# FNet and GeGLU layers on one core: the first row tiles' statistics and loads in another order, and the last rows' additions tied in turn

## The chip, the cores and the metric

One core of one Trainium2 chip. The metric is the device time of one execution in microseconds, the median of several runs. Profile times count from the first instruction of the profiled execution.

## The reference

Four layers over x (2048 rows of 512, fp32), each with a residual and a layer norm ahead of it: Fourier mixing, a GeGLU feed-forward layer, mixing again, feed-forward again.

```python
def _A_ref(x, dft_seq_re, dft_seq_im, dft_hid_re, dft_hid_im):
    a = jnp.einsum("bsd,ed->bse", x, dft_hid_re)
    b = jnp.einsum("bsd,ed->bse", x, dft_hid_im)
    return jnp.einsum("ts,bse->bte", dft_seq_re, a) - jnp.einsum("ts,bse->bte", dft_seq_im, b)
def _B_ref(x, w_gate, w_up, w_down):
    return (_gelu(x @ w_gate) * (x @ w_up)) @ w_down
x = A_x
x = x + _A_ref(_layernorm(x), ...)
x = x + _B_ref(_layernorm(x), ...)
x = x + _A_ref(_layernorm(x), ...)
x = x + _B_ref(_layernorm(x), ...)
```

The matrices are cosines and sines for the mixing (`ws` along the 2048 rows, `wh` along the 512 columns) and 512 x 1792 weights for the feed-forward layers.

## The kernel before

**Products.** Every fp32 operand is divided into a high part (rounded to fp32r by ScalarE, `split`, L126) and a low part (what is left, by VectorE, L128). A product is three matmuls (`mm3`, L166 to L168): high by high, high by low, low by high. Block products are saved in the manner of Strassen, which gives the many names (A11, S1, T2 and so on), and the additions for them run on VectorE (`minus` L154, `plus` L157) beside the matmuls.

**The opening.** In the first mixing layer the work goes over 16 half row tiles j and, in each, over 4 blocks b of output rows: `fore` calls `six` for each (j, b), and `six` takes the next divided 256 KB tile of `ws` (tile 4j + b), issues six matmuls of 512 columns with row tile j (24 a row tile), and then runs one entry of a work queue (`step`). Row tile j must by then be loaded (`x_load`, L194), normalised and divided. Normalising row tile i (`norm_terms`): VectorE's statistics (`bn_stats`, L531), mean and variance (L533), + EPS (L534), GpSimd's power -0.5 (L535), VectorE's shift (L536); then ScalarE writes the normalised row (`normed`, L572), and its halves are divided like the rest (`split_side`, which calls `split`). Row tiles 0 to 7 give the first eight j ("11"), and rows 8 to 15 are used for the other eight.

Row tile 0 has a function of its own, `first_tile` (statistics L1404, mean L1405, + EPS L1406, power L1407, subtraction L1408, high part L1411, low part L1412). It puts the division of ws tiles 0, 1 and 2 (`split_next`) around them. `first_made` and `issue_after` tie the divisions of tiles 1 and 2 behind row tile 0's own high and low part: `issue_after(ins)` keeps an instruction behind `ins` in the queue of the same engine.

Row tiles 1 to 7 come from the work queue: `opening(k)` asks for the load of row k + 1 and normalises row k, `first_parts(k)` divides it; after each pair stand as many pauses as `OPEN_GAPS` says, from the third pair on entries for rows 8 and up in their place. `opening(2)` (`SECOND_AT`) also asks for row 8. The statistics of a row are tied behind the + EPS step of the row before and the shift of the row before that (`terms_made`).

**Loads.** All loads of x and ws in the opening go through SyncE's queue (SP): x by L194, ws by `load_next`, L302. `split_next` keeps six ws tiles loaded ahead of the one that it divides (RAW), and `take`, which `six` calls, keeps seven divided ahead of the one used (AHEAD). An SP load uses one of eight semaphores in turn and waits until the load eight before it has landed.

**The order of the queues.** The code gives the dependences and an order of priority. The tile framework, with `schedule_with_timeline_sim`, plans each engine's queue at build on a timing model whose constants `machine_as_traced` sets; of what the model holds ready, it takes the earliest in the code. On the chip each queue runs as it was planned.

**The end.** In the last feed-forward layer `last_rows` computes the last product for four tiles of 128 rows: 21 matmuls of 256 columns for each (seven `mm3`), one addition to a tile `straight[n]` (loaded by L1292 from a scratch tensor, alternately on SP's and ScalarE's queue), and the store of the sum, 64 rows on SP's queue and 64 on ScalarE's (L1310).

Of the kernel before, what the change touches and what calls it, by code (L numbers as in the profile page):

```python
# [12 lines left out]
ALU = mybir.AluOpType  # L13

P = 128
S, D, F = 2048, 512, 1792
# [5 lines left out]
NT = TB // P  # L22
# [6 lines left out]
WARM = 11  # L29
OPEN_MORE = 0  # L30
SECOND_AT = 2
OPEN_GAPS = 1, 2, 1, 1, 1, 1, 1
NEAR = 2, 6
EARLY = 2
PACE = 9
# [26 lines left out]
def fnet_geglu(ctx: ExitStack, tc: tile.TileContext, x_in, ws, wh, whc, wgu, wdc, out):  # L62
    nc = tc.nc
# [57 lines left out]
    def f32(ap):  # L121
        return ap.bitcast(F32)

    def split(src, hi, lo):
        with behind(0):
            nc.scalar.activation(hi, src, AF.Copy)  # L126
        with behind(1):
            nc.vector.tensor_tensor(lo, src, f32(hi), op=ALU.subtract)  # L128

    first_made = []  # L130

    def behind(i):
        return tc.issue_after(first_made[i]) if first_made else nullcontext()
# [22 lines left out]
    def plus(out, a, b):  # L156
        nc.vector.tensor_tensor(out, a, b, op=ALU.add)  # L157
# [6 lines left out]
    def mm3(ps, a, b, start, stop):  # L164
        (ah, al), (bh, bl) = a, b
        nc.tensor.matmul(ps, ah, bh, start=start, stop=False, skip_group_check=True)  # L166
        nc.tensor.matmul(ps, ah, bl, start=False, stop=False, skip_group_check=True)  # L167
        nc.tensor.matmul(ps, al, bh, start=False, stop=stop, skip_group_check=True)  # L168
# [123 lines left out]
    def load_next():  # L292
        n = stream["loaded"]
        dtype, addresses, _, _ = items[n]
        raws[n] = []
        assert n not in needs or needs[n] in outside
        for a in addresses:
            t = sb.get(dtype)
            to = t if dtype == F32 else f32(t)
            if len(a.shape) == 3:  # L300
                to = to.rearrange("p (h c) -> p h c", h=2)
            stream["last"] = nc.sync.dma_start(to, a)  # L302
            raws[n].append(t)
        stream["loaded"] += 1

    def too_far(n):

        return items[n][2] is whole and n > stream["used"] + items[n][3]

    def split_next():  # L310
        n = stream["split"]
        while stream["loaded"] <= min(n + RAW, len(items) - 1) and not too_far(stream["loaded"]):
            load_next()
        parts[n] = items[n][2](*raws.pop(n))
        stream["split"] += 1

    def take():
        n = stream["used"]
        while stream["split"] < len(items):
            at = stream["split"]  # L320
            _, _, make, need = items[at]
            if too_far(at) or make is not whole and at > n + AHEAD + stream["more"]:
                break
            if make is not whole and need and need not in cs and at > n:
                break
            split_next()
        stream["used"] += 1
        return parts.pop(n)
# [183 lines left out]
    known, terms_made = {}, []  # L512

    def row_of(layer, i, mixed):
        x = fresh.pop(("mixed", i) if mixed else i, None)
        if x is None:
            x = (x_load_mixed if mixed else x_load)(layer, i)
        return x

    def norm_terms(layer, i, x, junk):  # L520

        pool = spool if layer == 0 else kpool
        rstd = pool.tile([P, 1], F32, name="rstd")
        shift = pool.tile([P, 1], F32, name="shift")
        if layer == 0:
            st = spool.tile([P, 6], F32, name="st")
            with ExitStack() as behind:
                for back, which in (1, 0), (2, 1):
                    if len(terms_made) >= back:
                        behind.enter_context(tc.issue_after(terms_made[-back][which]))  # L530
                nc.vector.bn_stats(st, x)  # L531
            mv = spool.tile([P, 2], F32, name="mv")
            nc.vector.bn_aggr(mv, st)  # L533
            added = nc.vector.tensor_scalar_add(rstd, mv[:, 1:2], EPS)  # L534
            nc.gpsimd.tensor_tensor(rstd, rstd, power, op=ALU.pow)  # L535
            made = nc.vector.scalar_tensor_tensor(shift, mv[:, 0:1], -1.0, rstd, op0=ALU.mult, op1=ALU.mult)  # L536
            terms_made.append((added.ins, made.ins))
        else:

            total = spool.tile([P, 1], F32, name="total")  # L540
            mean = spool.tile([P, 1], F32, name="mean")
            nc.scalar.activation(junk, x, AF.Copy, accum_out=total)  # L542
            nc.scalar.activation(mean, total, AF.Copy, scale=-1.0 / D)
            nc.scalar.activation(junk, x, AF.Square, bias=mean, accum_out=rstd)  # L544
            nc.gpsimd.tensor_scalar(rstd, rstd, 1.0 / D, EPS, op0=ALU.mult, op1=ALU.add)  # L545
            nc.gpsimd.tensor_tensor(rstd, rstd, power, op=ALU.pow)
            nc.scalar.activation(shift, mean, AF.Copy, scale=rstd)
        return rstd, shift
# [13 lines left out]
    def norm_begun(layer, i, mixed=False):  # L562

        x = row_of(layer, i, mixed)
        begun[layer, i] = x, known.pop((layer, i), None) or norm_terms(layer, i, x, junk)
# [516 lines left out]
    def geglu(w, layer):  # L1082
# [123 lines left out]
        def prepared(name, k):  # L1206

            if (name, k) in bs:
                return
            if name in ("S1", "S2") and len(h4[k]) == 4:  # L1210
                second_made(k)
            if name == "S2" and k >= MADE:
                fourth_made(k)
            t = h4[k][PLACE[name]]
            bs[name, k] = split_slot(t)
            sb.put(t)
# [60 lines left out]
        def halves(view, c):  # L1277
            return view[..., c * 64:(c + 1) * 64]
# [15 lines left out]
        def last_rows():  # L1294

            ks = range(NP)
            ts = [take()[0] for _ in ks]
            for k in ks:
                prepared("A22", k)
            to = xs[layer + 1, w * 2].rearrange("(n r) (p e) -> n r p e", r=P, e=P)  # L1300
            for n in range(NT):
                ps, v = ps8.get(), straight[n][:, :D // 2]
                for t, k in zip(ts, ks):
                    weights = (u[:, n * P:(n + 1) * P] for u in bs["A22", k])
                    mm3(ps[:, :D // 2], weights, (t[:, h] for h in half), k == 0, k == NP - 1)
                into = v.rearrange("r (p c e) -> r p c e", p=NT, e=32)
                plus(into, into, ps[:, :D // 2].rearrange("r (c p e) -> r p c e", p=NT, e=32))
                for i, engine in enumerate((nc.sync, nc.scalar)):
                    r = slice(i * 64, (i + 1) * 64)
                    engine.dma_start(halves(to[n, r], 1), v[r].rearrange("r (p e) -> r p e", e=64))  # L1310

        before_mix = w == 1 and layer < 3
# [41 lines left out]
        if last:  # L1354
            last_rows()
# [10 lines left out]
    ps = ps8.get()  # L1366
# [6 lines left out]
    def x_ahead(i):  # L1373
        if i < NS and i not in loaded:
            loaded.add(i)
            fresh[i] = x_load(0, i)
# [9 lines left out]
    def opening(k):  # L1386

        def run():
            x_ahead(k + 1)
            if k == SECOND_AT:  # L1390
                x_ahead(NK)
            first_norm(0, k)
        return run
# [7 lines left out]
    def first_tile():  # L1401

        x, st, mv, rstd = fresh.pop(0), *(spool.tile([P, n], F32, name=name) for name, n in (("st", 6), ("mv", 2), ("rstd", 1)))
        nc.vector.bn_stats(st, x)  # L1404
        nc.vector.bn_aggr(mv, st)  # L1405
        nc.vector.tensor_scalar_add(rstd, mv[:, 1:2], EPS)  # L1406
        nc.gpsimd.tensor_tensor(rstd, rstd, power, op=ALU.pow)  # L1407
        nc.vector.tensor_scalar(x, x, mv[:, 0:1], None, op0=ALU.subtract)  # L1408
        split_next()
        p = zparts["11", 0] = sb.get(F32R)  # L1410
        high = nc.scalar.activation(p[:, half[0]], x[:, half[0]], AF.Copy, scale=rstd)  # L1411
        made = nc.vector.scalar_tensor_tensor(p[:, half[1]], x[:, half[0]], rstd, f32(p[:, half[0]]), op0=ALU.mult, op1=ALU.subtract)  # L1412
        terms_made.append((made.ins, made.ins))
        first_made.extend((high.ins, made.ins))
        split_next()
        split_next()
        first_made.clear()

        def whole_row():
            z = za[0] = sb.get()  # L1420
            nc.scalar.activation(z, x, AF.Copy, scale=rstd)
            sb.put(x)
        return whole_row
# [6 lines left out]
    for n in range(NK - 1):  # L1430
        queue += [firsts.pop(0), firsts.pop(0)]
        queue += [seconds.pop(0) if n >= SECOND_AT else None for _ in range(OPEN_GAPS[n])]
    queue += seconds
# [77 lines left out]
```

## Time and profile before

| | before |
|---|---|
| time, median of 3 runs | 1589.22 us (1588.48 to 1590.95) |
| profiled execution, device time | 1589.32 us |
| profiled execution, span | 1587.3 us |
| VectorE busy, share of the span | 79% |
| ScalarE busy | 55% |
| GpSimd busy | 16% |
| DMA, mean over the span | 269 GB/s |
| granted TensorE clock | 0.999 |

The span runs from the first to the last instruction; the device time has 2.0 us more around it. A matmul's recorded duration overlaps with the next one's, so the distance from start to start is what counts. A row of the timeline may merge several instructions of a kind (x2, x9); its duration then runs from the start of the first to the end of the last. The bracket behind a row gives the idle time of the engine before it and what ended it. A DMA's row is its issue; landings are listed apart.

### The profile page before, as it was taken

Reading aid. Unit: us, or ns where it says so; the run is one execution under the profiler, and the core shown is the slowest. Engines: PE = TensorE matmul, PEld = TensorE weight load, DVE = VectorE, ACT = ScalarE, POOL = GpSimd, SP = SyncE. Lnnn points to the kernel's source line nnn. Section 1 sums busy time; section 2 is a strip of 40 time slices with the busy share of each in tenths; the row PEclk is TensorE's granted clock in tenths of the full one; section 3 lists DMA queues with packets and bytes.
Section 4 is the critical chain, followed back from the end, with each engine's and each line's share of the span. In section 5 each row is a group of like instructions: output and inputs, shape, how many; then the busy total and the mean of one; then the engine's idle time right before and its main releaser. Section 6 shows DMA issues by size and latency. Waiting matters only on the chain.

```text
span 1587.3 us, 23208 instructions
## 1 busy us (share of the span) xinstructions
PE 1579.0 (99%) x7000; PEld 1307.6 (82%) x7000; DVE 1250.1 (79%) x2174; ACT 875.4 (55%) x1714; POOL 253.6 (16%) x445
## 2 busy tenths in 40 slices
PE   9999999999999999999999999999999999999998
PEld 7888888888888888888888888888888888888887
DVE  8999999889699795566969997869985458754475
ACT  7864574645676652746768444566546435433361
POOL 2200324311465201230031000021002000000001
PEclk9999999999999999999999999999999999999999
DMA  9946989987999999996976785789998967896463
GB/s 360 332 150 232 361 270 362 335 286 259 328 344 345 297 329 301 288 331 221 310 238 217 270 229 172 233 283 309 279 327 239 297 198 238 293 289 197 135 197 81
DMA packets 257660, 427.04 MB, mean 269 GB/s; under 512 B 33344, under 2 KB 89408, under 8 KB 256512
## 3 DMA queue, kind: packets, MB, share of 16 engines
q1 hardware_dynamic: 228560, 333.28, 66.2%
q0 software_dynamic: 26544, 91.51, 15.7%
q8 instruction: 55, 0.90, 0.2%
q10 hardware_dynamic: 2432, 0.79, 0.2%
q14 instruction: 69, 0.57, 0.1%
HBM read 335.02 MB, written 90.44 MB: 268 GB/s over the span
## 4 chain that ended last, share of the span: by engine, by line
PE 96%; DVE 2%; DMA 2%; issue 0%; ACT 0%; SPq 0%; DVEq 0%; ACTq 0%
PE p L166 32%; PE p L167 32%; PE p L168 32%; DMA s<-ws 1%; DVE s L128 1%; DVE s L154 0%; DMA s<-x 0%; DVE s L157 0%; DVE xwide L154 0%; ACT s L126 0%; DVE wide L154 0%; SPq L302 0%; SPq L194 0%; ACT s L572 0%; DVE wide L157 0%
## 5 line engine op out<-in xcount | busy, mean ns | idle before, releaser
L167 PE MATMUL p<-s,s 128*128 128x512 f32 x2326 | 899.8, 388 | 0.0
L168 PE MATMUL p<-s,s 128*128 128x512 f32 x2326 | 887.6, 388 | 0.0
L166 PE MATMUL p<-s,s 128*128 128x512 f32 x2326 | 872.5, 388 | 2.0 <-ACT s L126 1.5
L126 ACT ACTIVATE s<-s 128x512 fp32r<-128x512 f32 (+1 forms) x868 | 487.4, 608 | 319.8 <-DVE s L154 108.7
L128 DVE TENSOR_TENSOR s<-s,s 128x512 fp32r<-128x512 f32 (+1 forms) x868 | 546.0, 669 | 58.2 <-ACT s L126 54.0
L166 PEld LDWEIGHTS p<-s,s 128*128 128x128 f32 x2326 | 436.7, 188 | 94.2 <-ACT s L126 3.4
L167 PEld LDWEIGHTS p<-s,s 128*128 128x128 f32 x2326 | 436.8, 188 | 89.7 <-DVE s L128 0.5
L168 PEld LDWEIGHTS p<-s,s 128*128 128x128 f32 x2326 | 436.6, 188 | 89.4
L157 DVE TENSOR_TENSOR s<-s,p 128x512 f32<-128x512 f32 (+1 forms) x293 | 196.2, 682 | 189.6 <-PE p L168 109.5
L154 DVE TENSOR_TENSOR s<-s,s 128x512 f32<-128x512 f32 (+1 forms) x414 | 249.8, 623 | 2.8 <-DMA s<-ws 0.9
L161 ACT ACTIVATE s<-p 128x512 f32<-128x512 f32 x252 | 146.9, 592 | 147.0 <-PE p L168 142.0
L1079 ACT ACTIVATE s<-s 128x512 f32<-128x512 f32 x112 | 70.3, 629 | 121.5 <-DVE s L157 121.0
L247 POOL DMA_DIRECT2D x<-wide x16 | 10.4, 660 | 374.7 <-DVE wide L157 374.7
L285 POOL DMA_DIRECT2D wb<-s x84 | 45.9, 548 | 100.2 <-ACT s L126 73.3
L1093 DVE TENSOR_TENSOR s<-s,s 128x512 f32<-128x512 f32 x84 | 57.9, 689 | 1.9
L126 ACT ACTIVATE s<-xwide 128x512 fp32r<-128x512 f32 (+1 forms) x52 | 31.0, 613 | 27.5 <-DVE xwide L157 10.0
L572 ACT ACTIVATE s<-s,shift,rstd 128x512 f32<-128x512 f32 x55 | 44.0, 807 | 3.9 <-DVE shift L536 3.2
L157 DVE TENSOR_TENSOR s<-s,s 128x512 f32<-128x512 f32 (+1 forms) x68 | 40.1, 591 | 5.0 <-DMA s<-wgu 3.3
L545 POOL TENSOR_SCALAR rstd<-rstd 128x1 f32<-128x1 f32 x48 | 14.2, 296 | 179.9 <-ACT junk L544 179.1
L285 POOL DMA_DIRECT2D wc<-s x42 | 30.1, 718 | 74.8 <-ACT s L126 53.2
L128 DVE TENSOR_TENSOR s<-xwide,s 128x512 fp32r<-128x512 f32 (+1 forms) x52 | 35.0, 682 | 7.1 <-ACT s L126 7.0
L542 ACT ACTIVATE junk<-s 128x512 f32<-128x512 f32 x45 | 28.1, 623 | 18.7 <-DMA s<-x 18.4
(105 smaller groups left out, 526.8 us busy)
## 6 DMA issues: line engine op xcount, KB each, us to landing
s<-ws SPq DMA_DIRECT2D x348, 256.0 KB, 5.1
s<-wb SPq DMA_DIRECT2D x294, 256.0 KB, 5.4
s<-wc SPq DMA_DIRECT2D x196, 256.0 KB, 4.5
wb<-s POOLq DMA_DIRECT2D x98, 256.0 KB, 5.6
s<-wp SPq DMA_DIRECT2D x56, 256.0 KB, 4.0
wc<-s POOLq DMA_DIRECT2D x49, 256.0 KB, 5.7
s<-x SPq DMA_DIRECT2D x45, 256.0 KB, 5.3
xwide<-x SPq DMA_DIRECT2D x43, 256.0 KB, 8.0
```

The source lines that it names most:

```text
L126: nc.scalar.activation(hi, src, AF.Copy)
L128: nc.vector.tensor_tensor(lo, src, f32(hi), op=ALU.subtract)
L154: nc.vector.tensor_tensor(out, a, b, op=ALU.subtract)
L157: nc.vector.tensor_tensor(out, a, b, op=ALU.add)
L161: nc.scalar.activation(v, src, AF.Copy)
L166: nc.tensor.matmul(ps, ah, bh, start=start, stop=False, skip_group_check=True)
L167: nc.tensor.matmul(ps, ah, bl, start=False, stop=False, skip_group_check=True)
L168: nc.tensor.matmul(ps, al, bh, start=False, stop=stop, skip_group_check=True)
L285: nc.gpsimd.dma_start(to, t)
L572: nc.scalar.activation(z, x, AF.Identity, bias=shift, scale=rstd)
L1079: nc.scalar.activation(t, g, AF.Gelu_apprx_tanh)
L1093: nc.vector.tensor_tensor(t, t, v, op=ALU.mult)
```

## The change

In the opening:

- `x_ahead` in `opening(k)` asks for row k + 2 (`X_AHEAD`) where it asked for row k + 1.
- The pauses after the first two pairs are 2 and 1 where they were 1 and 2.
- In `first_tile`, ws tile 1 is divided ahead of row tile 1's statistics, + EPS and shift (`norm_begun(0, 1)`, which were the first part of `opening(1)`); the statistics are tied behind tile 1's low part (`last_low`), and the low parts of the next two ws tiles, 2 and 3, behind row tile 1's + EPS step. `first_tile` now divides four ws tiles (0 to 3) and not three; `opening(1)` finds the terms begun and only writes the normalised row.

At the end:

- Each addition of `last_rows` is tied behind the one before it on VectorE.
- The rows of the first three tiles are stored whole by one DMA (ScalarE's, SP's and again ScalarE's queue), the last tile's as before in two halves.

```diff
-OPEN_GAPS = 1, 2, 1, 1, 1, 1, 1
+X_AHEAD = 2
+OPEN_GAPS = 2, 1, 1, 1, 1, 1, 1
...
         with behind(1):
-            nc.vector.tensor_tensor(lo, src, f32(hi), op=ALU.subtract)
-
-    first_made = []
+            last_low[0] = nc.vector.tensor_tensor(lo, src, f32(hi), op=ALU.subtract).ins
+
+    first_made, last_low = [], [None]
...
-                plus(into, into, ps[:, :D // 2].rearrange("r (c p e) -> r p c e", p=NT, e=32))
-                for i, engine in enumerate((nc.sync, nc.scalar)):
-                    r = slice(i * 64, (i + 1) * 64)
+                with tc.issue_after(made.ins) if n else nullcontext():
+                    made = nc.vector.tensor_tensor(into, into, ps[:, :D // 2].rearrange("r (c p e) -> r p c e", p=NT, e=32), op=ALU.add)
+                engines = (nc.sync, nc.scalar) if n == NT - 1 else ((nc.scalar, nc.sync)[n % 2],)
+                for i, engine in enumerate(engines):
+                    r = slice(i * P // len(engines), (i + 1) * P // len(engines))
                     engine.dma_start(halves(to[n, r], 1), v[r].rearrange("r (p e) -> r p e", e=64))
...
         def run():
-            x_ahead(k + 1)
+            x_ahead(k + X_AHEAD)
             if k == SECOND_AT:
                 x_ahead(NK)
             first_norm(0, k)
...
         made = nc.vector.scalar_tensor_tensor(p[:, half[1]], x[:, half[0]], rstd, f32(p[:, half[0]]), op0=ALU.mult, op1=ALU.subtract)
-        terms_made.append((made.ins, made.ins))
         first_made.extend((high.ins, made.ins))
+        split_next()
+        terms_made.append((last_low[0], last_low[0]))
+        norm_begun(0, 1)
+        first_made[1] = terms_made[-1][0]
         split_next()
         split_next()
         first_made.clear()
```

## The prediction

> **What bounds the kernel now.** I read first the busy times of the page, then TensorE's waits, then the timeline of the opening and of the end.
>
> ```profile
> span 1587.3 us, 23208 instructions
> ...
> PE 1579.0 (99%) x7000; PEld 1307.6 (82%) x7000; DVE 1250.1 (79%) x2174; ACT 875.4 (55%) x1714; POOL 253.6 (16%) x445
> ```
>
> TensorE's waits (total us, times, longest):
>
> ```profile
> PE p L166 <- ACT s L126: 1.5, 3, 0.8
> ```
>
> TensorE is the bound: idle 8.3 us of 1587.3, and the three waits of its matmuls for a high part (L126) sum to 1.5. So what the change can win lies in a few places: stalls in the opening, one later, and the stretch after the last matmul. The opening's timeline (start, duration, engine, line; the bracket is idle time before it):
>
> ```profile
> 7.52 0.62 PE L168 MATMUL p<-s,s 128*128 128x512 f32 x2
> ...
> 8.02 0.73 PE L166 MATMUL p<-s,s 128*128 128x512 f32 x2
> ...
> 9.97 0.40 PE L167 MATMUL p<-s,s 128*128 128x512 f32 x1
> ...
> 11.57 0.39 PE L168 MATMUL p<-s,s 128*128 128x512 f32 x1
> ...
> 12.71 0.50 PE L166 MATMUL p<-s,s 128*128 128x512 f32 x1 [0.75 <-ACT s L126]
> ...
> 23.54 0.39 PE L168 MATMUL p<-s,s 128*128 128x512 f32 x1
> ...
> 24.30 0.50 PE L166 MATMUL p<-s,s 128*128 128x512 f32 x1 [0.37 <-ACT s L126]
> ...
> 29.20 0.84 PE L168 MATMUL p<-s,s 128*128 128x512 f32 x3
> 29.99 0.50 PE L166 MATMUL p<-s,s 128*128 128x512 f32 x1
> 30.32 0.40 PE L167 MATMUL p<-s,s 128*128 128x512 f32 x1
> ```
>
> Durations overlap, so I count from start to start. Two matmuls take 0.62 where one takes 0.39: starts lie 0.23 apart. 11.57 to 12.71 is 1.14, so 0.91 is lost; the first gap after a stall is longer (29.99 to 30.32 is 0.33 to 0.34), 0.11 more. 23.54 to 24.30 loses 0.53, and 0.11 again. Before 29.99 it is 0.11 (the third of x3 starts at 29.20 + 0.45 = 29.65, the next was due at 29.88), then 0.11. At 8.02, due at 7.97, it is 0.05 and 0.11 (0.73 for two). **The opening can give 0.16 + 1.02 + 0.64 + 0.22 = 2.04 us, no more.** The stalls at 12.71, 24.30 and 29.99 stand before the first matmuls of row tiles 1, 3 and 4 (24 matmuls, 5.45 us, a row tile).
>
> **Row tile 1's statistics.** What made row tile 1 late:
>
> ```profile
> 5.88 0.62 ACT L126 ACTIVATE s<-s 128x512 fp32r<-128x512 f32 x1
> 6.00 0.48 DVE L1412 SCALAR_TENSOR_TENSOR s<-s,rstd,s 128x256 fp32r<-128x256 f32 x1 [0.40 <-ACT s L1411]
> ...
> 6.55 0.70 DVE L531 BATCH_NORM_STATS2 st<-s 128x6 f32<-128x512 f32 x1
> ...
> 7.16 0.67 DVE L128 TENSOR_TENSOR s<-s,s 128x512 fp32r<-128x512 f32 x1
> ...
> 7.75 0.17 DVE L533 BATCH_NORM_AGGREGATE mv<-st 128x2 f32<-128x6 f32 x1
> 8.00 0.69 DVE L128 TENSOR_TENSOR s<-s,s 128x512 fp32r<-128x512 f32 x1
> ...
> 8.61 0.15 DVE L534 TENSOR_SCALAR rstd<-mv 128x1 f32<-128x1 f32 x1
> ...
> 8.84 0.93 POOL L535 TENSOR_TENSOR rstd<-rstd,power 128x1 f32<-128x1 f32 x1 [3.41 <-DVE rstd L534]
> ...
> 10.49 0.63 ACT L126 ACTIVATE s<-s 128x512 fp32r<-128x512 f32 x1 [1.21 <-DMA s<-ws]
> 10.52 0.14 DVE L536 SCALAR_TENSOR_TENSOR shift<-mv,rstd 128x1 f32<-128x1 f32 x1
> ...
> 11.03 0.80 ACT L572 ACTIVATE s<-s,shift,rstd 128x512 f32<-128x512 f32 x1
> ```
>
> The chain is statistics, mean and variance, + EPS, the power on POOL, the shift, the normalised row on ScalarE (L572), its high half (L126), TensorE. Low parts (L128) stand between its short DVE steps. The change adds no instruction here. The low part of ws tile 1 goes first: its high part ends at 6.50, DVE is free at 6.48, so it starts at about 6.55 and the next 0.61 later (6.55 to 7.16 now). Then nothing stands between: statistics 7.16, mean about 7.87, + EPS 8.07. Behind that step, which was at 8.61, the low parts of tiles 2 and 3 now queue: about 8.15, where tile 2's was at 8.00, and 0.6 later. Tile 2's ends at 8.85, and its matmuls begin at 9.97 (the fifth L167), so this is hidden by 1.1 us, and a loss is excluded. POOL's power runs 8.3 to 9.2, and the shift comes behind tile 3's low part at about 9.4, 1.1 earlier than 10.52. ScalarE is idle from 9.28 (10.49 - 1.21) to 10.49, so L572 runs 9.6 to 10.4; its high half (0.40) follows at once, or behind tile 5's high part at 11.1 to 11.5. TensorE wants it at 11.80, or 11.64 without the 8.02 stall. **The first stall goes, 1.0 to 1.2 us**; tile 1's low part, 0.6 earlier, fills 8.02. What hides the moved work is that idle 1.21 of ScalarE. Were the row to stand behind the high parts of tiles 5 and 6, it would cost two of 0.62 again and the stall would stay.
>
> The Trainium skill ("TensorE: Matmul & The Clock Gate", Part 1: The HAM clock gate) says that ScalarE and VectorE take their queues strictly in order. By that rule L572 cannot pass a high part that waits for its load (10.49), and everything hangs on the planned order, as in rival A. This trace shows the wait of 1.21 us, but no ready instruction held behind it.
>
> **x rows two ahead.** What is late next is row tile 3:
>
> ```profile
> 13.17 0.33 SPq L194 DMA_DIRECT2D s<-x  x1
> ...
> 13.86 0.33 SPq L302 DMA_DIRECT2D s<-ws  x1
> ...
> 14.31 4.57 ACT L126 ACTIVATE s<-s 128x512 fp32r<-128x512 f32 x9
> ...
> 14.96 5.25 DVE L128 TENSOR_TENSOR s<-s,s 128x512 fp32r<-128x512 f32 x9 [0.28 <-ACT s L126]
> ...
> 20.11 0.69 DVE L531 BATCH_NORM_STATS2 st<-s 128x6 f32<-128x512 f32 x1
> ...
> 23.85 0.40 ACT L126 ACTIVATE s<-s 128x256 fp32r<-128x256 f32 x1
> ```
>
> The loads there (KB each, median us to landing):
>
> ```profile
> s<-x SPq DMA_DIRECT2D x15, 256.0 KB, 5.4
> ```
>
> SP issues one 256 KB load each 0.68 us (13.17, 13.86), and they land 5.4 later; row 3 landed at about 18.6. In the code its load stands behind ws tile 16 (asked for in row 2's opening); now, asked for in row 1's, behind tile 13. Three places of SP's queue are 2.0 us, and tiles 14 to 16 land 0.68 later each. That is hidden: ScalarE's nine high parts end at 18.88 with tile 16, which row tile 4 wants at 29.99. Rows 4 and 8, now asked for together behind tile 17, move 2.7 ahead and 0.7 back. The statistics of row 3 waited for nine operations of L128 (5.25, 0.58 each); two of these, the low parts of tiles 15 and 16, come behind it in code order, so with the row there it can start 1.15 earlier. Bounds: 0 (the same place in DVE's queue) and 2.0 (the whole lead); I take 1.15, from those rows. Its high half then ends at 24.25 - 1.15 = 23.1, where a TensorE without stalls wants it at 24.30 - (0.05 + 0.11 + 0.91 + 0.11 + 0.53) = 22.59. A stall of 0.5 is left, TensorE stands 1.15 earlier than now, and row tile 4 must come 1.15 earlier too, which its lead of 2.7 allows. With 0.1 to 0.2 of the 0.22 at 29.99 **the opening gives 1.3 us, bounds 0 and 2.04**. The gap of two, moved ahead, only shifts row 2's step by one group of six matmuls; row 2's tile is not late now: nothing.
>
> **The last rows.** The end:
>
> ```profile
> 1582.40 0.75 DVE L157 TENSOR_TENSOR s<-s,p 128x256 f32<-128x256 f32 x2 [3.80 <-PE p L168]
> ...
> 1582.86 1.47 ACTq L1310 DMA_DIRECT2D out<-s  x2
> ...
> 1583.53 0.80 ACTq L1310 DMA_DIRECT2D out<-s  x1
> ```
>
> The landing of these two issues of ACT's queue (last column, us), in their order:
>
> ```profile
> out<-s ACTq DMA_DIRECT2D x1, 64.0 KB, 2.9
> ...
> out<-s ACTq DMA_DIRECT2D x1, 64.0 KB, 2.7
> ```
>
> Stretches of the end (the last columns are TensorE's clock, the DMA engines' share, GB/s):
>
> ```profile
> 1581.50:1583.00 1.50, 0.87 (x8) 0.66 (x6) 0.59 (x2) 0.00 (x0) 0.00 (x0) 1.00 1.02 225
> 1583.00:1584.50 1.50, 0.00 (x0) 0.00 (x0) 0.16 (x1) 0.00 (x0) 0.00 (x0) 1.00 0.84 183
> ```
>
> DVE waits 3.80 us and then does two additions: row 2's had been ready for some 2.3 us (84 narrow matmuls, 0.12 each, 21 a row), but stood behind row 3's. Tied in turn, it runs at about 1580.1 and its one 128 KB store is issued then; row 3's runs at 1582.40 as now, and its halves, the last ones, issue at 1582.86 and not 1583.53. By the issue the last landing moves from 1583.53 + 2.7 to 1582.86 + 2.9, 0.47 earlier. But the DMA engines are at a share of 1.02 where row 2's bytes are pulled ahead to, and 0.84 just after; the same bytes drain, and only the unused 0.16 x 1.5 = 0.24 is surely to be had. Below: 0, if row 2's whole store holds up row 3's half on ACT's queue. I take **0.3**, nearer to 0.24.
>
> The Trainium skill ("DMA: Bandwidth & Descriptors", Queues, rings and completion order) says that the engines serve their queues in turn and each ring in order. By it the drain decides, and the end gains 0.24, not 0.47; the share of 1.02 agrees.
>
> **The sum.** 1589.32 (the profiled execution: its span of 1587.3 and 2.0 around it) - 1.3 - 0.3 = 1587.7. The median of the runs shown, 1589.22, is 0.1 lower, less than their spread. 0.2% is 3.2 us, about what a measurement of this kernel can tell from no change.
>
> **Rivals.** A, *the rows stay late* (0.24): the order of each queue is planned at build on a model of the chip, not taken from the code. If row 1's L572 is still planned behind tiles 5 and 6, or row 3's statistics behind the same low parts, the stall at 24.30 takes back what 12.71 gave. For it: row 3's statistics started 1.5 us after landing. Against: the code now puts both ahead. Opening 0.2, end 0.3: 1588.8. That the end keeps its order as well, so that the change does nothing: 1589.3 (0.06).
>
> B, *slower, by a new plan where VectorE has no reserve* (0.10):
>
> ```profile
> 880.00:922.00 42.00, 41.65 (x184) 34.22 (x183) 42.00 (x71) 21.73 (x37) 2.16 (x4) 1.00 0.73 236
> ```
>
> ```profile
> 920.34 0.47 PE L166 MATMUL p<-s,s 128*128 128x512 f32 x1 [0.35 <-ACT s L126]
> ```
>
> In the third layer DVE is busy 42.00 of 42.00 us, and TensorE stalls once (0.35 by its bracket; by starts about 0.5, as 0.37 was 0.53 at 24.30). 42.00 / 71 is 0.6 an operation. If the changed opening makes the planner put other DVE work ahead of what TensorE wants, each such operation costs 0.6. Three undo the gain; eight cost 4.8 and give 1587.7 + 4.8 = 1592.5, over 0.2% slower. For it: no reserve. Against: the code there is unchanged, and the stretch moves as a whole with TensorE.
>
> C, *all of it goes* (0.10): 2.04 in the opening, 0.47 at the end, the 0.5 at 920.34: 1589.32 - 3.0 = 1586.3. Even that is 0.18%.
>
> **How the numbers follow.** Forecast 0.50, A 0.24, nothing 0.06, B 0.10, C 0.10. Predicted 1587.7. Range 1586.3 to 1590.2: from C to the unchanged time and about 1 us, for the runs' spread and the first of B's operations; the rest of B and the lowest of C are left out. Faster by over 0.2% means under 1586.0, below what all stalls hold: 0.06, for the spread around C. Slower means over 1592.4, B alone: 0.10. Within: 0.84.
>
> **What would show it.** Right: the gap before 12.71 is gone and row tile 3 starts at about 23.1; statistics of row 3 at about 19.0; row 2's last addition alone near 1580.1 on the old scale, the last issue 0.46 us after the last addition's start, a span near 1585.7. Wrong: row 1's L572 still at 11.0; matmuls late at each row tile; new waits of TensorE between 880 and 922 us; a last landing as late after the last matmul as now, which would mean that the drain alone sets the end.

## The result, and the profile after

The changed kernel takes 1594.62 us (median of 18 runs, 1590.62 to 1596.88) against 1590.25 (18 runs, 1588.25 to 1594.34): ratio 1.0023, interval 1.0016 to 1.0029. The forecast was 1587.7, up to 1590.2. The profiled execution took 1595.86 us with a span of 1593.7, 1.2 above its median; that of before was 0.9 below its own, so the two profiles differ by 6.4 where the medians differ by 4.4.

The page of after: span and busy times.

```profile
span 1593.7 us, 23203 instructions
...
PE 1582.0 (99%) x7000; PEld 1308.6 (82%) x7000; DVE 1249.9 (78%) x2174; ACT 874.2 (55%) x1714; POOL 260.7 (16%) x445
```

Where the time went is read from the start of the same matmul in both traces:

| matmul (of 7000) | before, us | after, us | after is late by |
|---|---|---|---|
| 118, near row tile 4 | 29.99 | 28.38 | -1.61 |
| 770 | 177.93 | 176.30 | -1.63 |
| 900 | 207.60 | 210.24 | 2.64 |
| 2500 | 570.32 | 574.88 | 4.56 |
| 4000 | 910.32 | 915.72 | 5.40 |
| 5500 | 1251.02 | 1256.97 | 5.95 |
| 6999 | 1582.09 | 1587.97 | 5.88 |
| last landing | 1586.18 | 1592.42 | 6.24 |

The opening gained 1.6 us and TensorE kept it for 150 us. Then 4.3 us went between 176 and 210, 1.9 by 575, 1.4 by 1257, and 0.3 at the end. Of the 1.4, two gaps that before doesn't have, of 0.55 ending at 852.9 and of 0.43 ending at 1127.7, make 1.0.

A single profile of each kernel is a small sample. Four profiled kernels have the opening of before (before, e1, e9, e14 below): their matmul 118 starts at 29.45 to 30.59, mean 30.07. In the six with the changed opening (after, e2, e7, e11, e13, e17) it starts at 28.27 to 29.27, mean 28.64. By these the opening gained 1.4 us.

**The opening**, after: the timeline of TensorE, then of VectorE and ScalarE (start, duration).

```profile
11.33 0.39 PE L169 MATMUL p<-s,s 128*128 128x512 f32 x1
11.56 0.39 PE L167 MATMUL p<-s,s 128*128 128x512 f32 x1
...
22.44 0.40 PE L167 MATMUL p<-s,s 128*128 128x512 f32 x1
...
27.66 0.39 PE L169 MATMUL p<-s,s 128*128 128x512 f32 x1
28.38 0.50 PE L167 MATMUL p<-s,s 128*128 128x512 f32 x1 [0.33 <-ACT s L127]
```

```profile
7.10 0.69 DVE L532 BATCH_NORM_STATS2 st<-s 128x6 f32<-128x512 f32 x1
...
9.52 0.82 ACT L573 ACTIVATE s<-s,shift,rstd 128x512 f32<-128x512 f32 x1 [0.21 <-DVE shift L537]
...
17.34 0.69 DVE L532 BATCH_NORM_STATS2 st<-s 128x6 f32<-128x512 f32 x1
```

Row tile 1 starts at 11.56 without a gap (before 12.71 behind one of 0.91), row 3's statistics at 17.34 (20.11), row tile 3 at 22.44 (24.30); a stall of 0.49 + 0.11 is left, ahead of row tile 4.

**The first place of loss**, after: TensorE, then VectorE.

```profile
186.80 0.39 PE L169 MATMUL p<-s,s 128*128 128x512 f32 x1
188.99 0.98 PE L167 MATMUL p<-s,s 128*128 128x512 f32 x3 [1.80 <-ACT s L127]
...
190.60 0.63 PE L167 MATMUL p<-s,s 128*128 128x512 f32 x1
191.03 0.67 PE L168 MATMUL p<-s,s 128*128 128x512 f32 x1
```

```profile
179.57 0.69 DVE L129 TENSOR_TENSOR s<-s,s 128x512 fp32r<-128x512 f32 x1
184.61 0.69 DVE L158 TENSOR_TENSOR s<-s,s 128x512 f32<-128x512 f32 x1 [4.35 <-DMA s<-ws]
```

VectorE does nothing from 180.26 to 184.61: an addition at the head of its queue waits for a ws tile. What follows, down to the high part that TensorE wants, is late: a gap of 2.19 from start to start, 1.96 lost, and then matmuls 0.43 apart. The stretch shows the clock (last columns: granted clock, DMA share, GB/s), after and before:

```profile
190.00:195.00 5.00, 5.00 (x16) 3.76 (x16) 4.91 (x9) 2.53 (x5) 0.00 (x0) 0.67 1.03 362
```

```profile
190.00:195.00 5.00, 5.00 (x23) 3.98 (x22) 5.00 (x9) 3.14 (x6) 0.00 (x0) 1.00 1.05 387
```

The DMA engines are full here in both kernels. In before, VectorE's waits for ws at this place sum to 1.8 us, and TensorE doesn't notice (total, times, longest; between 160 and 196):

```profile
DVE s L157 <- DMA s<-ws: 1.8, 2, 1.0
```

The awaited tile is the fifth of a burst of ws loads in before (it lands at 182.38) and the sixth in after (184.59); each is some 1.8 us behind the one ahead of it.

**The second place**, 473 to 484 us: TensorE waits 1.2 us for an addition, and this for a load of the next weights, in after:

```profile
DVE s L158 <- DMA s<-wgu: 3.0, 1, 3.0
```

and in before:

```profile
DVE s L157 <- DMA s<-wgu: 1.0, 1, 1.0
```

What made that load late stands 35 us ahead, in a group that I had not looked at: POOL's first statistic instruction on 128x1 (busy us, mean ns), before and after.

```profile
L545 POOL TENSOR_SCALAR rstd<-rstd 128x1 f32<-128x1 f32 x48 | 14.2, 296 | 179.9 <-ACT junk L544 179.1
```

```profile
L546 POOL TENSOR_SCALAR rstd<-rstd 128x1 f32<-128x1 f32 x48 | 20.1, 419 | 185.7 <-ACT junk L545 185.0
```

48 equal instructions, and 5.9 us more: nearly all of it is one of them. POOL's timeline after:

```profile
437.88 5.96 POOL L546 TENSOR_SCALAR rstd<-rstd 128x1 f32<-128x1 f32 x1 [5.35 <-ACT junk L545]
443.93 0.57 POOL L547 TENSOR_TENSOR rstd<-rstd,power 128x1 f32<-128x1 f32 x1
444.45 0.61 POOL L286 DMA_DIRECT2D wb<-s  x1
```

and before:

```profile
434.95 0.20 POOL L545 TENSOR_SCALAR rstd<-rstd 128x1 f32<-128x1 f32 x1 [5.01 <-ACT junk L544]
435.23 0.63 POOL L546 TENSOR_TENSOR rstd<-rstd,power 128x1 f32<-128x1 f32 x1
435.82 0.61 POOL L285 DMA_DIRECT2D wb<-s  x1
```

POOL's writes of weight parts queue behind it and come in a crowd later, into the loads of 455 to 475: from 440 to 450 us the DMA engines' share is 0.64 (1.03 before), and from 450 to 460, where POOL is busy 9.24 of 10 us (5.94 before), it is 1.01 (0.89).

**The end**, after: the last stores (KB each, us to landing).

```profile
out<-s ACTq DMA_DIRECT2D x2, 128.0 KB, 6.2
out<-s SPq DMA_DIRECT2D x1, 128.0 KB, 6.7
out<-s SPq DMA_DIRECT2D x1, 64.0 KB, 3.4
out<-s ACTq DMA_DIRECT2D x1, 64.0 KB, 3.7
```

As forecast, row 2's addition runs alone (1586.02), and the last issue follows 0.45 us behind the last addition's start. But the last halves land 3.4 and 3.7 us after their issue, not 2.7 and 2.9: from the start of the last matmul to the last landing it is 4.44 us, 4.10 before.

### The profile page after: what moved, and what is told of

Same layout as the page of the kernel before. It is cut to its first block, busy times and chain, and to the rows that moved or that the text cites. A ratio compares the mean times of both kernels' runs of the same rounds, so it can differ in the third digit from the quotient of the medians.

```text
span 1593.7 us, 23203 instructions
## 1 busy us (share of the span) xinstructions
PE 1582.0 (99%) x7000; PEld 1308.6 (82%) x7000; DVE 1249.9 (78%) x2174; ACT 874.2 (55%) x1714; POOL 260.7 (16%) x445
## 4 chain that ended last, share of the span: by engine, by line
PE 46%; ACT 2%; issue 1%; DMA 1%; DVE 0%; POOL 0%; SPq 0%; POOLq 0%; ACTq 0%; DVEq 0%
PE p L167 15%; PE p L169 15%; PE p L168 15%; ACT s L127 1%; DMA s<-x 0%; ACT junk L545 0%; DMA s<-ws 0%; ACT s L573 0%; ACT junk L543 0%; POOL rstd L547 0%; DVE s L158 0%; ACT shift L548 0%; ACT xwide L162 0%; ACT s L162 0%; DVE s L129 0%
## 5 line engine op out<-in xcount | busy, mean ns | idle before, releaser
L158 DVE TENSOR_TENSOR s<-s,p 128x512 f32<-128x512 f32 x289 | 195.0, 687 | 182.6 <-PE p L169 106.0
L546 POOL TENSOR_SCALAR rstd<-rstd 128x1 f32<-128x1 f32 x48 | 20.1, 419 | 185.7 <-ACT junk L545 185.0
L573 ACT ACTIVATE s<-s,shift,rstd 128x512 f32<-128x512 f32 x55 | 44.2, 809 | 4.1 <-DVE shift L537 2.8
```

Of the source, the lines that this page charges most:

```text
L573: nc.scalar.activation(z, x, AF.Identity, bias=shift, scale=rstd)
```

## The experiments

Each was measured over five rounds; the ratio is to the kernel before on the same chip. A "gap" is the time from one matmul's start to the next, less the usual 0.23. "Two ahead" means X_AHEAD = 2.

**e1: the last rows' edits alone.** The opening as before.

> The kernel before with the change's last rows alone: additions tied in turn, three whole stores. Theory P (the loss is a new planned order after the opening, from x rows two ahead): this kernel keeps every queue's order of before up to the last rows, so no new TensorE waits and a time within 0.5 us of before, gain or loss (the profile of the changed kernel has the end 0.5 us longer, from last matmul to end, 5.4 against 4.9). Theory E (the end costs): 1 us or more slower than before, with the last landing over 3.5 us after its issue.

Ratio 1.0008 [0.9999, 1.0016]; 4.80 us from the last matmul to the last landing. The edits don't gain.

**e2: the whole opening change, the old last rows.**

> The whole change of the opening, the last rows as before. Theory P: 4 to 6 us slower than before, TensorE's stalls of the opening down from 2.0 to 0.7 us, and new ones near 179 to 193 us and 473 us. Theory E: 1 us or less slower.

1.0024 [1.0013, 1.0034]: the opening carries the loss, with gaps of 0.4 to 1.1 at 176 to 208, 0.9 at 472 and 0.8 at 1106.

**e3: only row tile 1's statistics moved.** X one ahead, old pauses.

> Row tile 1's statistics and tile 1's low part first, but x rows one ahead and the pauses 1, 2 as before. Its queues are those of before from about 50 us on. Theory P: no new stalls; TensorE's gap before row tile 1 is gone (1.2 us), part of it comes back at row tile 3, and the time is 0 to 1.2 us below before. Rival O (moving the statistics itself upsets the later order): 3 us or more slower.

0.9998 [0.9989, 1.0006]. Row tile 1's gap goes, 0.73 comes back ahead of row tile 3, and the lead left at matmul 770, 0.77, is lost at 181 to 207.

**e4: two ahead and the new pauses, without the statistics.**

```diff
+X_AHEAD = 2
+OPEN_GAPS = 2, 1, 1, 1, 1, 1, 1
...
+            x_ahead(k + X_AHEAD)
```

> x rows two ahead and the pauses 2, 1 alone, the statistics where they were. Theory P: this part alone brings the new order of loads, so it is 4 to 7 us slower than before, with the stalls near 179 to 193 us and 473 us. Rival O: within 1 us of before.

1.0030 [1.0021, 1.0040]. The profiled execution is the longest of the ten (1598.64, median 1594.52). Here TensorE is 1.04 us *later* than in before at matmul 770, and still has a gap of 1.54 at 189. So the gap doesn't need a lead of TensorE that VectorE fails to follow; what is left is the plan of the queues after the opening.

**e5: the pauses alone (2, 1).**

> The kernel before with the pauses 2, 1 alone (x rows one ahead). Its planned queues differ from those of before until about 200 us and then not again; the load that the first addition of the second block waits for (the second ws tile of its sixth group) stands sixth in its burst, as in the changed kernel, where before has it fifth. Theory L (a load's place in SP's queue in the full DMA stretch of 165 to 195 us sets TensorE's stall there, one place 1.8 us): a stall of 1 to 3 us near 185 to 191 us, none near 473 us, 1 to 3 us slower than before. Rival T (TensorE's earlier start alone makes the stall, since the landings stay where they are): no TensorE lead here, so no stall and a time within 0.7 us of before.

0.9994 [0.9986, 1.0003]: a miss. The awaited ws tile is the sixth here too, and there is no gap: the burst begins at 165.15 us and not at 168.11, and the tile lands at 181.63. The place in the burst is not enough. Its start goes with the landing as well, and SP's load ahead of the burst waits until a write of POOL has landed (at 168.39 in before, 166.97 in after, about 163.5 here).

**e6: two ahead alone.**

> x rows two ahead alone, the pauses 1, 2 as before. Its planned queues differ up to about 560 us, and the tile stands fifth. Theory L: no stall over 0.7 us near 185 to 191 us, but the new order near 473 us is there, with 1 to 1.5 us of stalls; 1.5 to 3 us slower than before with what the opening adds. Rival T: as e4_xahead, 4 to 5 us slower.

1.0008 [0.9999, 1.0017], one execution of 6664 us aside. No gap at 176 to 210, one of 1.11 at 470.2. The cost is below the 1.5 to 3 us that were expected.

**e7: e2, and nine ws loads tied in code order,** which puts the awaited tile second.

```diff
+            with tc.issue_after(stream["turn"].ins) if n in in_turn and "turn" in stream else nullcontext():
+                stream["last"] = nc.sync.dma_start(to, a)
...
+                        if layer == 0 and b == 1 and k in (5, 6, 7):
+                            in_turn.add(len(items))
```

> The whole change of the opening, the last rows as before, and three groups of ws loads (of block 1's fifth stage, nine loads from the sixth group on) tied to stand in SP's queue in the order of the code; the tile moves from the sixth to the second place of its burst, and the queues are otherwise those of the change of the opening alone. Theory L: the stalls of 179 to 193 us (2.7 us in the run without the tie, with their restarts) fall under 0.7, those at 473 us stay; 2 to 3 us faster than without the tie, that is 0.5 to 1.5 us slower than before. If the tile's slot is free too late, SP waits there and nothing is gained. Rival T: stalls as without the tie.

1.0016 [1.0006, 1.0027]. The gaps at 187 to 193 are gone, and VectorE waits for no ws load from 160 to 196 us, so the awaited load made them. By time it is 0.0008 less than e2, 1.3 us where 2 to 3 were expected, and the two intervals overlap. Gaps of 1.06 at 178.5, 1.9 at 470 and 1.2 at 1104 stay.

**e8: e3 with the same tie.**

> Row tile 1's statistics first (x rows one ahead, pauses as before, last rows as before) and the same tie of nine loads. Theory L: TensorE keeps its lead of 0.7 to 1.2 us through 165 to 195 us, no stall over 0.3 us there, and no new plan after 200 us: 0.7 to 1.5 us faster than before, the fastest version so far. Rival T: the lead is lost at 181 to 194 us as without the tie, a time equal to before.

1.0007 [0.9997, 1.0016]: a miss. A lead of 1.06 us at matmul 770 is lost at 179.6 (1.60).

**e9: the additions of the last rows tied, the stores left in halves.**

> The kernel before, with the four last additions tied in turn and every last row still stored in two halves on two queues; the whole stores are left as they were. From the last matmul's start to the end the trace of before has 5.17 us, the whole edit of the last rows 5.72 and 6.06. Theory W (the whole stores of 128 KB cost, the tie gains): the tail is 4.7 to 5.0 us, last row's addition directly behind its last matmul, time 0.2 to 0.5 us under the kernel before, ratio 0.9997 to 0.9999. Rival: the tie itself costs, because the rows 0 to 2 give up their places to the order: tail 5.6 to 6.1, time 0.5 to 0.9 above, ratio 1.0003 to 1.0006. Rival: neither, tail 5.1 to 5.3, ratio 1.0000 within 0.0005, and then the halves' number alone or the two edits together made the loss.

1.0002 [0.9993, 1.0012], 4.21 us from the last matmul to the last landing: no effect of the tie is seen.

**e10: e6, and one statistic off POOL.** Layer 2's row tile 12 is the one that took 5.97 us in e6.

```diff
-            nc.gpsimd.tensor_scalar(rstd, rstd, 1.0 / D, EPS, op0=ALU.mult, op1=ALU.add)
+            if (layer, i) == (1, 12):
+                nc.scalar.activation(rstd, rstd, AF.Copy, scale=1.0 / D, bias=EPS)
+            else:
+                nc.gpsimd.tensor_scalar(rstd, rstd, 1.0 / D, EPS, op0=ALU.mult, op1=ALU.add)
```

> X rows two ahead alone (as in the run with that name's edit, 0.5 us over the kernel before, with a TensorE gap at 470.2 us of 1.1 us over a matmul), and one statistic instruction moved: the scale and EPS of row tile 12 in the second layer goes from POOL to ScalarE. In the run without it this POOL instruction (128x1) took 5.97 us at 434.7 against 0.20 in before, beside an unbroken string of VectorE additions with two SBUF operands, and POOL issued its next writes 5.4 us later than in before; the planned order of SP, VectorE and TensorE stays the same in all but a few places around it. Theory S (the starved POOL instruction makes the writes late, these crowd the loads of wgu at 455 to 470, VectorE's addition waits for them): the writes behind it issue at 435 to 437, the addition's wait for wgu falls from 2.8 to about 1 us, no TensorE gap above 0.3 us at 465 to 485, time 1.0 to 1.9 us lower than that run, so ratio 0.9993 to 0.9997 against the kernel before. The power on POOL may starve in its place: then it shows about 6 us and the gap stays, which tells nothing against S. Rival P (the planned order of the loads makes them late, whatever POOL does): gap of 1 us and more stays though POOL's instructions are short, ratio 1.0003 to 1.0008.

0.9992 [0.9983, 1.0001]. POOL's writes, which stood behind the 5.97 us in e6 (first at 441.23), now go ahead:

```profile
434.93 0.54 POOL L286 DMA_DIRECT2D wb<-s  x1 [6.07 <-ACT s L127]
435.93 0.73 POOL L286 DMA_DIRECT2D wc<-s  x1 [0.46 <-ACT s L127]
```

VectorE's wait, 2.8 us in e6, is

```profile
DVE s L158 <- DMA s<-wgu: 1.3, 1, 1.3
```

and no gap is left between 14 and 900 us. The time is 0.0016 below e6. The starved instruction was the cause of the second place.

**e11: e7 with the same statistic moved.**

> The whole opening change with the old last rows and the nine ws loads tied (1.0016 in the run without the next edit), and the same statistic of row tile 12 moved from POOL to ScalarE. Theory S: the gap at 470 (1.9 us in all) goes, 1.3 to 1.9 us less than without: ratio 1.0004 to 1.0008; the gap at 178.5 (1.1 us) stays. Rival P: ratio stays 1.0013 to 1.0019, gap at 470 stays.

1.0001 [0.9992, 1.0009]: 0.0015 less than e7, no gap at 470. The profiled execution is the longest of the eleven (1593.22, median 1589.75); it has gaps of 1.6 at 180 and of 1.6 at 1104.

**e12: statistics and pauses, x one ahead.**

> Row tile 1's statistics ahead and the pauses 2, 1, with x rows one ahead as in before and the old last rows. Behind the opening the planned order is that of the pauses alone (0.9994, no gap of 0.2 us between 100 and 400 us, VectorE 13.7 us busy of 15 in 165 to 180). Theory: the lead that the statistics give is handed back at 179 to 182 us only where VectorE is full there (15.0 of 15 with statistics alone); here VectorE has a reserve, so the lead of 1.0 to 1.2 us lasts: no gap at 175 to 185, idx 900 at about 206.4 to 206.8 us, 0.8 to 1.3 us under the pauses alone, ratio 0.9985 to 0.9991. Rival: the reserve is small, or what waits there is a load whose landing doesn't come earlier: the lead is lost again, 0.5 us and more of gaps at 176 to 195, ratio 0.9992 to 1.0000.

0.9994 [0.9986, 1.0003], where 0.9985 to 0.9991 was expected. No gap at 175 to 185, as expected, but row tile 3 pays 1.28 at 22.2; matmul 900 starts at 206.43, 1.17 ahead of before. The lead lasts, the opening isn't better than in the other runs.

**e13: the changed kernel with e10's edit.**

> The changed kernel itself (opening and last rows), with one instruction moved: the scale and EPS of row tile 12's statistics in the second layer from POOL, where it took 5.96 us at 437.9 in the profile of after, to ScalarE. SP's order differs in 16 places, TensorE's in 123, all of them around it. Theory S (a third of the loss is this starved instruction): no TensorE gap above 0.3 us at 465 to 490, where after has 1.9 us in all; the changed kernel's 1.0023 falls by 0.0009 to 0.0016, to 1.0007 to 1.0014. Rival P (the loads' order): 1.0020 to 1.0026, gap at 470 to 475 stays.

1.0025 [1.0014, 1.0036]: a miss. In the profiled execution the gaps at 470 are gone, but it is the shortest of the eight (1591.47, median 1593.31); it still loses 0.98, 0.54, 0.42 and 0.42 at 180 to 209. What the longer ones lose beside that no profile shows.

**e14: the first three last rows stored whole, their additions not tied.**

> The kernel before, with the first three last rows stored whole on one queue each, their additions not tied. The tie alone left the time from the last matmul's start to the last landing at 4.21 us (4.10 in before, 4.07 to 4.45 in nine kernels with the old last rows), and both edits together have 4.80 and 4.44. Theory W (the whole 128 KB stores are what costs): 4.5 to 4.9 us here, ratio 1.0002 to 1.0008. Rival (the two together, or the scatter of one profile): 4.1 to 4.4, ratio 0.9996 to 1.0002.

1.0004 [0.9996, 1.0013], 3.98 us from last matmul to last landing: neither edit alone costs by this measure. Unlooked for, the statistic starved here too, although the plan is that of before up to the last rows:

```profile
436.65 4.35 POOL L545 TENSOR_SCALAR rstd<-rstd 128x1 f32<-128x1 f32 x1 [4.96 <-ACT junk L544]
```

and a gap of 0.85 follows at 472; this execution is 2.1 us above the median. So it isn't decided by the plan alone. The traces show what goes with it. VectorE's next addition begins 59 to 66 ns after POOL's instruction in the seven profiles in which that instruction took 0.19 to 0.20 us (before, e1, e3, e5, e8, e9, e12), 67 ns after it in e14, and 127 to 135 ns after it in the six with two ahead that had it on POOL, where it was held. What divides them at some 66 ns is not shown.

**e15: statistics, two ahead, old pauses and last rows, and e10's edit.**

> X rows two ahead and row tile 1's statistics ahead, without the new pauses, old last rows, and the one statistic moved to ScalarE. Theory (the loss is the order at 165 to 195 that the pauses and the two rows ahead make together, and the starved POOL instruction; neither is here): no gap over 0.3 us from 40 to 800 us but for what VectorE hands back at 180, opening 0.7 to 1.3 us ahead of before, ratio 0.9984 to 0.9992. Rival (the lead of the statistics is given back at 176 to 195 us here too): idx 900 no earlier than 206.6 us, as in the run with two rows ahead and the moved statistic alone, ratio 0.9990 to 0.9998.

0.9992 [0.9983, 1.0001], one execution of 4145 us aside. Opening 2.2 us ahead of before (27.78 at matmul 118); gaps of 0.2 and 0.4 are left at 185 to 188, where VectorE waits 2.3 us for ws.

**e16: e6, and one VectorE instruction of 128x1 with one SBUF operand** in the string of additions.

```diff
+            if (layer, i) == (1, 12):
+                one = spool.tile([P, 1], F32, name="one")
+                nc.vector.tensor_scalar_add(one, junk[:, :1], 0.0)
```

> X rows two ahead alone, POOL's statistics left where they were, and one 128x1 VectorE instruction added that reads one operand of SBUF; its result isn't used. It stands in VectorE's order behind the first addition that follows POOL's instruction at 434.7, in the unbroken string of additions with two SBUF operands (434.8 to 440.6), and TensorE's order is unchanged. Theory S (POOL's instruction waits until VectorE issues one without a second SBUF operand, as it did until the transpose at 440.5): POOL's instruction ends at the added one, in 0.5 to 1.2 us instead of 5.97, its writes issue 4 to 5 us earlier unless the power after it is held in the same way for some 5 us; no gap at 465 to 485 then, ratio 0.9990 to 0.9997. Rival Q (POOL's instruction is slow for a reason of its own, the string is coincidence): 5.9 us again, gap of 1 us and more at 470, ratio 1.0003 to 1.0010.

1.0014 [1.0005, 1.0022]. POOL, then VectorE's two instructions of one operand, the added one (L548) and the transpose that stands in the code:

```profile
433.65 0.87 POOL L549 TENSOR_SCALAR rstd<-rstd 128x1 f32<-128x1 f32 x1 [5.34 <-ACT junk L545]
434.60 5.45 POOL L550 TENSOR_TENSOR rstd<-rstd,power 128x1 f32<-128x1 f32 x1
```

```profile
434.38 0.15 DVE L548 TENSOR_SCALAR one<-junk 128x1 f32<-128x1 f32 x1
...
439.53 0.70 DVE L667 STREAM_TRANSPOSE wide<-s 128x512 f32<-128x512 f32 x1
```

The first POOL instruction ends at 434.52 with the added one (434.53). The second, begun behind it, is held for 5.45 us and ends in the transpose. This is theory S with the proviso that its expectation named; that POOL's instruction is slow for a reason of its own has fallen. Writes and loads are late as in e6, and TensorE pays more:

```profile
469.17 0.39 PE L169 MATMUL p<-s,s 128*128 128x512 f32 x1
472.23 0.69 PE L167 MATMUL p<-s,s 128*128 128x512 f32 x1 [2.67 <-DVE s L158]
472.73 0.63 PE L168 MATMUL p<-s,s 128*128 128x512 f32 x1
```

**e17: the changed kernel with both edits,** the tie of e7 and the statistic of e10.

> The changed kernel itself with both edits: the nine ws loads of one block tied in turn, and the statistic of row tile 12 moved from POOL to ScalarE. The first alone took 0.0008 off the opening change, both together 0.0023 (1.0024 to 1.0001, with the old last rows); the second alone took nothing off the changed kernel (1.0025 against 1.0023). Theory (two causes, and the order of the ws loads has to go first): 1.0000 to 1.0008, the rest over 1.0001 being the last rows; no gap over 0.5 us at 185 to 195 and at 465 to 490, one of 1 us and more at 178 to 182 left. Rival (a third cause in the changed kernel that neither edit touches): 1.0016 to 1.0028 as with the second edit alone.

0.9999 [0.9990, 1.0009]: the loss is gone. Against e13, which differs from it by the tie alone, it is 0.0026 less, and the two intervals don't meet. TensorE's waits by the profile (total, times, longest): only the one near 180 is left, beside the start.

```profile
PE p L168 <- DVE s L129: 1.5, 1, 1.5
```

**e18: e15 with the tie,** the fastest.

> Statistics ahead, x rows two ahead, old pauses, old last rows, the statistic on ScalarE (0.9992 so far, with gaps of 0.2 and 0.5 us at 185 to 188 where VectorE waits 2.3 us for ws loads), and the nine ws loads tied in turn. Theory (the place of the ws loads makes those gaps): they go, 0.5 to 0.9 us less than without the tie, ratio 0.9984 to 0.9990. Rival (the tie brings the awaited load forward and others back, and the lead is given back near 180 as in the two runs with the tie before): 0.9991 to 1.0000, a gap of 0.5 us and more at 176 to 183.

0.9984 [0.9975, 0.9993], 1587.46 us (12 runs) against 1589.75. VectorE waits for nothing between 165 and 196 us, matmul 900 starts at 205.60, 2.0 ahead of before, and TensorE has no gap over 0.1 us from 14 to 800.

```profile
span 1586.1 us, 23224 instructions
...
PE 1578.6 (100%) x7000; PEld 1307.6 (82%) x7000; DVE 1249.3 (79%) x2174; ACT 876.0 (55%) x1715; POOL 257.0 (16%) x444
```

## Why the prediction was wrong

**Row tile 1's statistics: right.** 1.0 to 1.2 us, measured 1.15 (12.71 to 11.56; by the means of the four and the six profiles named above, 1.0). The steps came within 0.2 us of those forecast (shift 9.33, L573 9.52).

**x rows two ahead: right within the opening, too small.** Row 3's statistics start 2.77 us earlier, beyond the bound of 2.0; the stall left is 0.49, as forecast, but before row tile 4. In all 1.61 for 1.3 (bounds 0 and 2.04), or 1.4 by the means.

**The last rows: wrong.** The additions and issues moved as forecast and the end did not come earlier. Fourteen kernels with the old last rows have 4.07 to 4.45 us from the last matmul to the last landing (mean 4.24), the four with both edits 4.80, 4.44, 4.38 and 4.45. So -0.3 became about +0.3, though three of the four lie within the range of the old ones: that it got worse is not clear, but a gain of 0.3 is in none of them. The prediction named this sign: a last landing as late after the last matmul as before would mean that the drain sets the end. Not even the 0.24 of free share was to be had.

**The sum: the step that failed.** It added the opening and the last rows and put all that lies between at nothing; the one reason given, against rival B, was that the code there is unchanged and "the stretch moves as a whole with TensorE". It didn't move as a whole: in the two profiles 7.9 us were lost behind the opening (from 1.63 ahead to 6.24 late). The x loads asked for one row earlier, with one pause moved, changed the planned order of SP's loads in over fifty places, counting only those where a load of another kind now stands; the last is at 545 us, of 1587. The kernel's DMA-full stretches have little reserve, and two of them turned against it:

- at 165 to 195 us the awaited ws tile lands 2.2 us later. Shown by e7, where the tie removes these gaps, by e18, where VectorE's waits for ws go with it, and by e17 against e13 (0.0026 of the time). None of the five profiles with the tie has a gap over 0.2 us from 183 to 210 us.
- at 434 to 444 us POOL's statistic of row tile 12 meets VectorE's string of additions. Shown by e10 and e11 (0.0016 and 0.0015 of the time) and by e16.

Both edits together take the changed kernel from 1.0023 to 0.9999 (e17). They don't add: the second alone took nothing off it (e13) and 0.0015 off the one with the tie.

**Rival B: right in kind, wrong in place and means.** A new plan met a stretch without reserve, but at 180 and 470 us through transfers, not at 880 to 922 through a displaced VectorE addition at 0.6 each; that its price of 4.8 us is near the 4.4 measured is luck, since it was made of eight displaced operations. (C's 3.0 us are 0.19%, not 0.18.) VectorE's busy share, by which I chose the place, doesn't tell: in before it is 15.00 of 15 us at 165 to 180, as full as at 880 to 922, but 6.97 of 10 at 460 to 470. What had no reserve was the landing of loads, in VectorE's waits of 1.8 and 1.0 us that ended just in time. They stood among VectorE's waits of before, and both times it was at a wait that cost nothing yet that the new plan cost.

**My first theory fell.** It held that the tile's place in the burst alone decides; e5 has it sixth without a gap. Nor was it the lead of TensorE (e4). **Open** stay: what the longer executions of e13 lose; what divides the held POOL instruction from the one of 0.20 us at some 66 ns; and the gap of 1.6 us near 180 in e8, e11 and e17, a low part of VectorE that is late, which e18 doesn't have.

A third place shows in the traces, and no experiment was made on it. Near 1080 to 1093 us VectorE's transpose waits until the write `t<-wide` has landed. It waits 3.6, 4.0, 4.4 and 5.6 us in e2, e7, e11 and e4, where TensorE then has gaps of 0.8, 1.2, 1.6 and 2.8 us at 1104 to 1108; in the sixteen other profiles it waits 1.6 to 3.3 (2.3 in before, 2.1 in after), and no gap over 0.6 follows there. As e4's and e11's profiles are of their longest executions, this may be part of what long executions lose; for e13 it isn't shown.

## What to carry to other kernels

An edit of the opening of a planned kernel can change the plan far behind it, here up to a third of the way: list, ahead of it, the waits in the DMA-full stretches that end just in time, and compare the planned queues before and after. If the gain vanishes later, look at the same matmul in both traces to find where, and then at groups of equal instructions whose total differs: the 5.9 us in 48 of them led to the cause. Then tie the few loads that matter, or move the instruction that starves, instead of undoing the edit.

## What the runs showed of the hardware that I had not expected

- A POOL instruction on 128x1 that elsewhere takes 0.2 to 0.6 us was held for 4.35 to 5.97 us beside an unbroken string of VectorE additions with two SBUF operands: in the profiles of all five kernels with two ahead that had it on POOL and were not otherwise altered (after, e2, e4, e6, e7: 5.96 to 5.97), in e14 and, as the power, in e16. Each time it ended within the first VectorE instruction of one operand, but in e14, where it ended near 441.0 as one addition began only when the last had ended. The Trainium skill ("SBUF — State Buffer", Who interferes with whom) says that VectorE with two SBUF inputs contends with GpSimd reading SBUF, and calls the port pair that they share an exclusive lock. The trace agrees on who contends; the hold lasted over a string of some 13 instructions, not one, and in before the same instruction got through such a string in 0.20 us (e14 above has the distances that go with the two kinds).
- A gap of 2.19 us between matmul starts was followed by matmuls 0.43 us apart from 189.8 to 193.2 (granted clock 0.67 in 190 to 195), one of 3.06 us in e16 by the same from 472.7 to 475.7. In after this cost 1.6 us on top of the 1.96 of the gap. But one of 3.0 us in e4, at 1108.2 to 1111.2, was followed at once by matmuls 0.23 apart at a granted clock of 1.00, and one of 2.1 in e7 by matmuls 0.24 apart: the length alone doesn't decide it. The Trainium skill ("TensorE: Matmul & The Clock Gate", Part 1: The HAM clock gate) gives an idle window of about 3.4 us; these gaps were shorter, and the slow stretches were 3.0 to 3.4 us long.
- In the full stretch at 168 to 178 us a 256 KB load took 9.2 us to land (median of seven, after; 8.8 before), where all ws loads of the run have 5.1.
